# First batch of the attention: diagonal-scaled transposes, V stationary, x produced transposed

## The chip, the cores and the metric

The kernel runs on one core of one Trainium2 chip, as a single program. Engines are named as in the profile: PE (TensorE matmuls), PEld (its weight loads), DVE (VectorE), ACT (ScalarE), POOL (GpSimd) and SP (SyncE, here a DMA queue). The metric is the device time of one execution in microseconds (us), as the median over runs; the kernel before takes 684.7 us (three runs, 682.42 to 688.06).

## What is computed

Three stages follow one another: a banded attention, a SiLU feed-forward network, and a mixture of eight experts of which each token uses one. The change touches the attention alone (2 batches, 8 heads, 768 positions, 64 columns a head; the first 8 key positions are seen by all queries, and each query sees 96 positions back):

```python
scores = scale * np.matmul(q, k.transpose(0, 1, 3, 2)) + bias     # bias falls with distance
scores = np.where(keep, scores, -1000000000.0)
a = np.exp(scores - np.max(scores, axis=-1, keepdims=True))
a = a / (np.sum(a, axis=-1, keepdims=True) + 1e-09)
x = np.matmul(a, v)                       # then x: (1536 tokens, 512) goes on
h = x @ w_in
g = h * (1.0 / (1.0 + np.exp(-h)))
x = g @ w_out                             # then the experts
```

## The kernel before, in words

The 1536 tokens are 12 tiles of 128; tiles 0 to 5 are the first batch, tiles 6 to 11 the second. The attention of a tile is done in four steps of two heads each, called slots: slot s is tile s//4, head pair s%4. The first batch is slots 0 to 23 (`SB=24`) and runs ahead of everything else, by `slot_b`; the second batch runs between the matmuls of the feed-forward network, by `slot`, and isn't touched.

A pair of heads goes through a pipeline over four slots. In slot s the code issues, in this order (the instructions of an engine run in the order in which they are issued, under `manual_schedule`):

- `emit_tr` for slot s-2: four PE transposes against the identity (two heads, two key blocks of 128; tile 0 has one block, so two transposes), then ACT's copy of the result to SBUF (L187);
- `emit_tb` for the first head of slot s: DVE adds the bias table to the scores and takes the row maximum (L159);
- `emit_exp` for slot s-1: two ACT exponentials with row sums in `ss` (L169);
- one step of the decoding of a weight (`dec_op`, DVE, from slot 8 on; the weights arrive as 64-bit words and three DVE steps make them 32-bit);
- `emit_tb` for the second head, and `emit_mx`, which scales the maximum (L162); then `emit_qk` for slot s+1: the scores of two heads, each a float32 matmul over 64 rows and 256 columns (L150);
- `glob_k` (POOL copies the global keys, L138), then `emit_pv` for slot s-3: four float32 matmuls in which the transposed weights are the stationary operand and 64 columns of V stream (L197). They fill `pvt[n]`, 128 tokens by 512.

When a tile's fourth pair is through, `emit_rs` makes the inverse sums on DVE (L206, L207), `emit_fin` multiplies `pvt` by them into `xa` (DVE, L211), and one slot later `emit_xt` transposes `xa` by four PE transposes (L218); ACT copies that to `xT` (L222), and DVE makes the rest of the split of `xT` into two float32r parts (L223). The feed-forward network reads `xT` as its streaming operand (L292).

PSUM banks of the pipeline come in turn from five (`abank`, L112). A float32 matmul that isn't a transpose shows in the trace as two instructions (88 matmuls at L197 give 176 rows, 48 at L150 give 96), a transpose as one. POOL also computes the bias tables in the first slots (`tab_heads`, L109, in slots 1, 2, 4, 5, 6, 9 by `TAB`). `WPL` (L40) holds the slots after which nine loads of weights are issued on the SP queue.

The first feed-forward matmul (L292) follows slot 23 on PE. Slots 24 to 26, which only finish the pipeline, stand between the matmuls of its first steps. In those steps DVE decodes the weights that are left.

Of the kernel before, what the change touches and what calls it, by code (L numbers as in the profile page):

```python
# [10 lines left out]
F32 = mybir.dt.float32  # L11
# [5 lines left out]
AF = mybir.ActivationFunctionType  # L17
ALU = mybir.AluOpType
AX = mybir.AxisListType
P = 128  # L20
# [3 lines left out]
def kernel(ctx, tc, qk, v, n_global, n_local, w_in, w_out, wg, w1, w2, out):  # L24
    nc=tc.nc
    B,NT=v.shape[0],v.shape[1]
    H=8; D=64; KC=4; FB=16; NTT=B*NT; LAG=2; LASTF=2; HB=6; PAIR=256; PX=4
# [4 lines left out]
    SB=24  # L32
# [4 lines left out]
    WL=4  # L37
    LOPB=(1,2,3)
    LATE=(0,1)
    WPL=(2,4,6,8,10,12,14,17,20)  # L40
    WPS=(12,15,18,21,23)
    TAB=(1,2,4,5,6,9)
    const=ctx.enter_context(tc.tile_pool(name="const",bufs=1,side="left"))
# [1 line left out]
    attn=es_a.enter_context(tc.tile_pool(name="attn",bufs=1,side="right"))  # L45
# [11 lines left out]
    ident=const.tile([P,P],F32,name="ident")  # L57
# [4 lines left out]
    def own_first(n): return n%3==1  # L62
# [76 lines left out]
    def glob_v(n):  # L139
        if n%NT in (0,NT-1): return  # L140
        if 4*n<SB: G.tensor_copy(vpr4[0:32,n%3,0:512],vpr4[0:32,(n-1)%3,0:512])
        else: V.tensor_copy(vpr[0:32,n%3],vpr[0:32,(n-1)%3])
# [8 lines left out]
    def emit_tb(n,hp,j):  # L151
        i=n%NT; h=2*hp+j; q=qp.pop((n,hp,j))
        if j==0: tt[n,hp]=attn.tile([P,2,2,P],F32,tag="t",name="t",bufs=3)
        t=tt[n,hp]
        if h==0:
            mx[n]=attn.tile([P,H],F32,tag="mx",name="mx",bufs=2); ss[n]=attn.tile([P,H],F32,tag="ss",name="ss",bufs=2)
        sl=slice(0,2) if i else slice(0,1)
        tb=tabs[:,3:4,h,:] if i==0 else (tabs[:,1::-1,h,:] if i==1 else tabs[:,1:3,h,:]) if own_first(n) else tabs[:,0:2,h,:] if i==1 else tabs[:,2:0:-1,h,:]
        V.tensor_tensor_reduce(out=t[:,j,sl],in0=q[:,sl],in1=tb,scale=1.0,scalar=-3e38,op0=ALU.add,op1=ALU.max,accum_out=mx[n][:,h:h+1])  # L159
    def emit_mx(n,hp):  # L160
        h=2*hp+1
        V.tensor_scalar(out=mx[n][:,h-1:h+1],in0=mx[n][:,h-1:h+1],scalar1=-0.125,scalar2=float(np.log(1024.0)),op0=ALU.mult,op1=ALU.add)  # L162
    def emit_exp(n,hp):
        i=n%NT
        t=tt[n,hp]
        ce=1 if i==0 else 2
        for j in range(2):
            h=2*hp+j
            A.activation(out=t[:,j,:ce],in_=t[:,j,:ce],func=AF.Exp,scale=0.125,bias=mx[n][:,h:h+1],accum_out=ss[n][:,h:h+1])  # L169
# [4 lines left out]
    def emit_l(n,hp):  # L174
        t=tt.pop((n,hp)); x=hl.pop((n,hp)); nch=ce=1 if n%NT==0 else 2
        (G if hp in LOPB else V).tensor_tensor(out=x[:,:,1],in0=t[:,:,:ce],in1=x[:,:,0],op=ALU.subtract)
        y=attn.tile([P,2,2,nch,P],F16,tag="pT",name="pT",bufs=3)
        pT[n,hp]=y
        S.dma_start_transpose(out=y.rearrange("p a b c d -> p (a b c) d"),in_=x.rearrange("p a b c d -> p (a b c d)"))
    def emit_tr(n,hp):  # L180

        t=tt.pop((n,hp)); ce=1 if n%NT==0 else 2
        m=abank([P,2,ce,P],"tp")
        for j in range(2):
            for c in range(ce): T.transpose(m[:,j,c],t[:,j,c],ident)
        y=attn.tile([P,2,ce,P],F32,tag="pT",name="pT4",bufs=3); pT[n,hp]=y
        A.activation(out=y,in_=m,func=AF.Copy)  # L187
    def emit_pv(n,hp):
        i=n%NT; ce=1 if i==0 else 2
        if hp==0: pvt[n]=ps.tile([P,H,D],F32,tag="pv" if 4*n>=SB or n%2 else "s1",name="pv",bufs=1)  # L190
        y=pT.pop((n,hp))
        vb=[n%3] if ce==1 else [n%3,(n-1)%3] if own_first(n) else [(n-1)%3,n%3]
        for j in range(2):
            h=2*hp+j
            for c in range(ce):
                if 4*n<SB:
                    T.matmul(pvt[n][:,h,:],y[:,j,c,:],vpr4[:,vb[c],h*D:(h+1)*D],start=(c==0),stop=(c==ce-1))  # L197
                    continue
                seq=[(0,0),(0,1),(0,2),(1,0),(1,1)]
                for k,(a,m) in enumerate(seq):  # L200
                    T.matmul(pvt[n][:,h,:],y[:,j,a,c,:],vpr[:,vb[c],m,h*D:(h+1)*D],start=(c==0 and k==0),stop=(c==ce-1 and k==4))
    rs={}
    def emit_rs(n,k):
        if k==0:
            rs[n]=attn.tile([P,H,1],F32,tag="rs",name="rs",bufs=2)
            V.tensor_scalar(out=rs[n][:,:,0],in0=ss[n],scalar1=1024.0e-9,scalar2=None,op0=ALU.add)  # L206
        else: V.reciprocal(out=rs[n],in_=rs[n])  # L207
    def emit_fin(n):
        r=rs.pop(n)
        xa=attn.tile([P,H,D],F32,tag="hl" if 4*n<SB else "t",name="xa",bufs=2 if 4*n<SB else 3)  # L210
        V.tensor_tensor(out=xa,in0=pvt[n],in1=r.to_broadcast([P,H,D]),op=ALU.mult)  # L211
        xas[n]=xa
    xas={}
    def emit_xt(n):
        xa=xas.pop(n)
        m=abank([P,KC,P],"ms")
        for k in range(KC):
            T.transpose(m[:,k,:],xa[:,2*k:2*k+2,:].rearrange("p a d -> p (a d)"),ident)  # L218
        c,u=divmod(n,2)
        if u==0: xT[c]=mp.tile([P,2,KC,256],F32R,tag="xT",name="xT",bufs=3)  # L220
        sl=xT[c][:,:,:,u*P:(u+1)*P]
        A.activation(out=sl[:,0],in_=m,func=AF.Copy)  # L222
        V.tensor_tensor(out=sl[:,1],in0=m,in1=sl[:,0],op=ALU.subtract)  # L223
# [616 lines left out]
    def slot_b(s):  # L840

        ev=[]
        n,hp=divmod(s,4); n1,h1=divmod(s-1,4); n2,h2=divmod(s-2,4); n3,h3=divmod(s-3,4)
        def a_():
            if s<SB-3: want(min(s+WL,SB-1))
            elif s<SB: want(s+3)
            if 0<=s-2<SB: emit_tr(n2,h2)
            if s==0:
                for j in range(2): emit_qk(n,hp,j)
            if s<SB: emit_tb(n,hp,0)  # L850
            if 0<=s-1<SB: emit_exp(n1,h1)
        ev.append(a_)
        def a2():
            if s<SB: emit_tb(n,hp,1); emit_mx(n,hp)
            if s+1<SB:
                for j in range(2): emit_qk(*divmod(s+1,4),j)
        ev.append(a2)
        def b_():
            if s<SB: glob_k(n,hp)
            if 0<=s-3<SB:  # L860
                emit_pv(n3,h3)
                if h3==3: glob_v(n3)
            if h3==3 and 0<=s-3<SB: emit_rs(n3,0); emit_rs(n3,1)
            if fin: emit_xt(fin.pop())
            if s==0: table(slice(0,3))
            for k in range(2):
                if s==TAB[k]:
                    for h in range(4*k,4*k+4): tab_heads(slice(0,2),slice(0,2),(h,))
            for k in range(4):
                if s==TAB[2+k]:  # L870
                    for h in range(2*k,2*k+2): tab_heads(slice(2,3),slice(2,3),(h,))
        ev.append(b_)
        def e2():
            if h3==3 and 0<=s-3<SB: emit_fin(n3); fin.append(n3)
            if hp==3 and n+1<NTT and s<SB: load_v(n+1)
        ev.append(e2)
        return ev
# [144 lines left out]
```

## Time and profile before

| what | value |
|---|---|
| median of 3 runs | 684.7 us |
| the profiled execution, its own time | 692.54 us |
| its span, first to last instruction | 690.7 us |
| PE busy | 647.9 us (94%) |
| PE weight loads | 541.4 us (78%) |
| DVE busy | 384.3 us (56%) |
| ACT busy | 303.3 us (44%) |
| POOL busy | 204.8 us (30%) |

The page gives each engine's busy time and the share of the span. A view by stretches gives busy time, granted clock and DMA share of chosen microseconds. The timeline gives instructions in order of time, equal neighbours merged into one row with their count; the difference of two rows' starts is what the first one cost the engine. A matmul's recorded length overlaps its neighbour's, so on PE starts are read and not lengths.

### The profile page before, as it was taken

To read this page: it belongs to the slowest core of one execution; us is meant where nothing else is said; L and a number is where in the kernel's file an instruction comes from. 1 tells how busy PE (TensorE), PEld (TensorE's weight loads), DVE (VectorE), ACT (ScalarE), POOL (GpSimd) and SP (SyncE) were. 2 spreads that over 40 slices of the span, in tenths; PEclk is the share of its full clock that TensorE was granted. 3 is DMA by queue.
4 is the path that set the end of the run, shared out by engine and by line. 5 is a ranking of instruction groups with operands and counts; after the bars stand their busy time and mean duration, and the time that the engine had idled before them with its cause. 6 is when DMAs were issued, how large, how long until landed. Compare 5 with 4: busy or idle time off the path is not lost. (4 is left out here: it accounts for less than half of the span.)

```text
span 690.7 us, 11869 instructions
## 1 busy us (share of the span) xinstructions
PE 647.9 (94%) x3990; PEld 541.4 (78%) x3990; DVE 384.3 (56%) x1013; ACT 303.3 (44%) x789; POOL 204.8 (30%) x230
## 2 busy tenths in 40 slices
PE   2999998999989989999999999889799999999995
PEld 1677787888878868888888989778688888888883
DVE  3344444999963555555535334474274387779750
ACT  2444444334434434433343232444266376766641
POOL 5412120344421133212211101172443244434311
PEclk9999999999999999999999999999899999999998
DMA  7132223377433788547355735951685456776600
GB/s 256 34 106 78 76 76 127 120 222 217 159 115 105 81 165 169 138 93 167 93 129 92 131 92 76 245 164 31 198 267 177 154 175 216 238 264 220 215 18 18
DMA packets 83671, 98.75 MB, mean 143 GB/s; under 512 B 35547, under 2 KB 49883, under 8 KB 83602
## 3 DMA queue, kind: packets, MB, share of 16 engines
q1 hardware_dynamic: 76850, 86.69, 46.5%
q0 software_dynamic: 3312, 8.08, 3.6%
q10 hardware_dynamic: 3440, 3.15, 1.5%
q8 instruction: 33, 0.54, 0.3%
q14 instruction: 36, 0.29, 0.1%
HBM read 81.85 MB, written 11.52 MB: 135 GB/s over the span
## 5 line engine op out<-in xcount | busy, mean ns | idle before, releaser
L292 PEld LDWEIGHTS s<-xT,wi 128*128 128x128 f32 x1152 | 150.6, 194 | 19.2 <-DVE g L301 12.3
L292 PE MATMUL s<-xT,wi 128*128 128x256 f32 x1152 | 156.3, 288 | 6.3 <-DVE g L301 5.4
L297 DVE SCALAR_TENSOR_TENSOR s<-u,s 128x256 f32<-128x256 f32 x96 | 39.8, 426 | 104.1 <-ACT u L296 103.7
L296 ACT ACTIVATE u<-s 128x256 f32<-128x256 f32 x96 | 35.2, 380 | 114.3 <-PE s L292 110.5
L307 PE MATMUL s<-woh,g 128*128 128x512 f32 x192 | 81.8, 426 | 0.0
L458 DVE TENSOR_TENSOR uq<-qr,uq 128x512 fp32r<-128x512 f32 x81 | 76.3, 957 | 8.0 <-ACT uq L457 4.4
L308 PE MATMUL s<-woh,g 128*128 128x512 f32 x192 | 77.7, 405 | 0.0
L150 PE MATMUL qkp<-ring 64*128 64x256 f32 (+1 forms) x192 | 60.0, 543 | 15.1 <-DMA ring<-in_qk_dram 12.3
L457 ACT ACTIVATE uq<-qr 128x512 fp32r<-128x512 f32 x112 | 66.4, 625 | 7.6 <-DMA qr<-in_w_dram 7.6
L301 DVE TENSOR_TENSOR g<-s,g 128x256 fp32r<-128x256 f32 x96 | 39.3, 422 | 31.8 <-ACT g L300 24.0
L458 POOL TENSOR_TENSOR uq<-qr,uq 128x512 fp32r<-128x512 f32 x31 | 41.0, 1331 | 53.8 <-ACT uq L457 50.3
L300 ACT ACTIVATE g<-s 128x256 fp32r<-128x256 f32 x96 | 35.7, 380 | 47.2 <-DVE s L297 46.7
L607 PE MATMUL y<-uq,hh 128*128 128x512 f32 (+6 forms) x136 | 55.7, 410 | 0.0
L608 PE MATMUL y<-uq,hh 128*128 128x512 f32 (+6 forms) x136 | 54.0, 397 | 0.0
L609 PE MATMUL y<-uq,hh 128*128 128x512 f32 (+6 forms) x136 | 54.0, 397 | 0.0
L309 PE MATMUL s<-wolr,g 128*128 128x512 f32 x128 | 52.0, 406 | 0.2 <-DMA wolr<-wlo_d 0.2
L150 PEld LDWEIGHTS qkp<-ring 64*128 64x128 f32 x192 | 26.8, 247 | 30.2 <-DMA ring<-in_qk_dram 9.9
L197 PEld LDWEIGHTS pv<-vpr,pT 128*128 128x128 f32 x176 | 36.9, 308 | 13.0 <-issue 13.0
L169 ACT ACTIVATE t<-t,mx 128x256 f32<-128x256 f32 (+1 forms) x96 | 45.7, 480 | 0.4 <-DVE mx L162 0.4
L599 ACT ACTIVATE hh<-h 128x224 fp32r<-128x224 f32 (+6 forms) x64 | 23.3, 363 | 49.6 <-DVE h L597 29.0
L307 PEld LDWEIGHTS s<-woh,g 128*128 128x128 f32 x192 | 37.5, 195 | 9.5 <-ACT u L296 1.7
L600 DVE SCALAR_TENSOR_TENSOR hh<-h,hh 128x224 fp32r<-128x224 f32 (+6 forms) x64 | 25.3, 395 | 32.6 <-ACT hh L599 29.6
(211 smaller groups left out, 1134.2 us busy)
## 6 DMA issues: line engine op xcount, KB each, us to landing
qr<-in_w_dram SPq DMA_DIRECT2D x128, 256.0 KB
wolr<-wlo_d SPq DMA_DIRECT2D x64, 256.0 KB
wiraw<-in_w_in_dram SPq DMA_DIRECT2D x16, 512.0 KB
wraw<-in_w_out_dram SPq DMA_DIRECT2D x13, 512.0 KB
wlo_d<-wol SPq DMA_DIRECT2D x16, 256.0 KB
xs<-xr SPq DMA_DIRECT2D x6, 513.0 KB
ring<-in_qk_dram SPq DMA_DIRECT2D x12, 256.0 KB
ring<-in_qk_dram ACTq DMA_DIRECT2D x10, 256.0 KB
```

Source lines behind the costliest of these rows:

```text
L150: T.matmul(q[:,sl],w[:,z,1],w[:,z:z+1,0] if i==0 else w[:,0:3:2,0] if z==0 else w[:,z-1:z+1,0],start=True,stop=True)
L169: A.activation(out=t[:,j,:ce],in_=t[:,j,:ce],func=AF.Exp,scale=0.125,bias=mx[n][:,h:h+1],accum_out=ss[n][:,h:h+1])
L292: T.matmul(t,w[:,ww,kc,:],x[:,xx,kc,:],start=(k==0),stop=(k==11)); k+=1
L297: V.scalar_tensor_tensor(out=t,in0=u,scalar=1.0,in1=t,op0=ALU.add,op1=ALU.mult)
L307: T.matmul(s2p[u][k],g[:,0,sl],wh,start=(f==0),stop=False)
L308: T.matmul(s2p[u][k],g[:,1,sl],wh,start=False,stop=False)
L309: T.matmul(s2p[u][k],g[:,0,sl],wl,start=False,stop=(f==FB-1))
L457: A.activation(out=t[:,0],in_=r,func=AF.Copy)
L458: (G if (i%2 if pool is None else pool) else V).tensor_tensor(out=t[:,1],in0=r,in1=t[:,0],op=ALU.subtract)
L607: T.matmul(o,g[:,0,sl],w[:,0],start=(f==0),stop=False)
L608: T.matmul(o,g[:,1,sl],w[:,0],start=False,stop=False)
L609: T.matmul(o,g[:,0,sl],w[:,1],start=False,stop=(f==7))
```

## The change

It concerns the first batch alone.

- New `emit_dg` for slot s-1, issued in slot s behind `emit_mx`: DVE adds the constant to the two row sums and inverts them (two small instructions a slot), and POOL multiplies the identity by each head's inverse sums, one 128 by 128 instruction a head: a diagonal matrix `dg`, float32, in two buffers.
- `emit_tr` no longer transposes against the identity: it is an ordinary float32 matmul with the exponentials as the stationary operand and `dg` streaming. What comes out is the transposed weights, already divided by their sums. ACT's copy of it is issued behind the exponentials of slot s-1 and no longer ahead of them.
- `emit_px` takes the place of `emit_pv`: V (64 columns) is the stationary operand, the transposed weights (128 columns) stream. The two heads of a pair write to partitions 0 to 63 and 64 to 127 of the same PSUM columns, in turn. x comes out transposed, tile by tile, and goes to `xT` at once by `put_xt` (the ACT copy and the DVE subtraction as before, read from the matmul's own bank).
- Gone from the first batch: `emit_rs`, `emit_fin` and the four transposes of `emit_xt` for each of six tiles.
- `WPL`: the loads of weights on the SP queue come up to two slots later.

```diff
-    WPL=(2,4,6,8,10,12,14,17,20)
+    WPL=(4,6,8,10,12,14,16,18,20)
...
+    def emit_dg(n,hp):
+        s=ss[n][:,2*hp:2*hp+2]
+        V.tensor_scalar(out=s,in0=s,scalar1=1024.0e-9,scalar2=None,op0=ALU.add)
+        V.reciprocal(out=s,in_=s)
+        d=attn.tile([P,2,P],F32,tag="hl",name="dg",bufs=2); dg[n,hp]=d
+        for j in range(2): G.tensor_scalar(out=d[:,j],in0=ident,scalar1=s[:,j:j+1],scalar2=None,op0=ALU.mult)
...
-            for c in range(ce): T.transpose(m[:,j,c],t[:,j,c],ident)
+            for c in range(ce): T.matmul(m[:,j,c],t[:,j,c],d[:,j],start=True,stop=True)
...
-        A.activation(out=y,in_=m,func=AF.Copy)
+        return y,m
+    def emit_px(n,hp):
+        i=n%NT; ce=1 if i==0 else 2
+        if hp==0: pvt[n]=ps.tile([P,KC,P],F32,tag="pv" if n%2 else "s1",name="px",bufs=1)
...
+        for c in range(ce):
+            for j in range(2):
+                h=2*hp+j
+                T.matmul(pvt[n][j*D:(j+1)*D,hp,:],vpr4[:,vb[c],h*D:(h+1)*D],y[:,j,c,:],start=(c==0),stop=(c==ce-1))
+    def emit_xx(n):
+        put_xt(n,pvt[n])
...
-                    T.matmul(pvt[n][:,h,:],y[:,j,c,:],vpr4[:,vb[c],h*D:(h+1)*D],start=(c==0),stop=(c==ce-1))
...
-            if 0<=s-2<SB: emit_tr(n2,h2)
+            if 0<=s-2<SB: y,m=emit_tr(n2,h2)
...
             if 0<=s-1<SB: emit_exp(n1,h1)
+            if 0<=s-2<SB: A.activation(out=y,in_=m,func=AF.Copy)
...
             if s<SB: emit_tb(n,hp,1); emit_mx(n,hp)
+            if 0<=s-1<SB: emit_dg(n1,h1)
...
-                emit_pv(n3,h3)
-                if h3==3: glob_v(n3)
-            if h3==3 and 0<=s-3<SB: emit_rs(n3,0); emit_rs(n3,1)
-            if fin: emit_xt(fin.pop())
+                emit_px(n3,h3)
+                if h3==3: glob_v(n3); emit_xx(n3)
...
-            if h3==3 and 0<=s-3<SB: emit_fin(n3); fin.append(n3)
```

The order on PE around the end of a tile, in the middle of the first batch. The names are the tiles written and read; a count behind a row counts matmuls of the code. Before:

```order
L150 MATMUL qkp<-ring_78 128x256 x2
L197 MATMUL pv<-vpr,pT_383 128x64 x4
L218 MATMUL ms<-ident,xa 128x128 x4
L185 MATMUL tp<-ident,t 128x128 x4
L150 MATMUL qkp<-ring_78 128x256 x2
L197 MATMUL pv<-vpr,pT_412 128x64 x4
```

And with the change:

```order
L150 MATMUL qkp<-ring_78 128x256 x2
L204 MATMUL px<-pT_416,vpr 64x128 x4
L193 MATMUL tp<-dg,t 128x128 x4
L150 MATMUL qkp<-ring_78 128x256 x2
L204 MATMUL px<-pT_447,vpr 64x128 x4
```

The four transposes of `xa` are gone; the transposes of the weights have become matmuls against `dg`, and the product with V has changed its operands' places.

The order on POOL in the first slots, before (the tables of L109 stand together):

```order
L109 TENSOR_SCALAR tabs<-wk 128x128 x6
L109 TENSOR_SCALAR tabs<-wk 128x2x128 x8
L138 COPY ring_78<-ring_78 128x32
L109 TENSOR_SCALAR tabs<-wk 128x128 x2
L138 COPY ring_78<-ring_78 128x32
```

And with the change:

```order
L109 TENSOR_SCALAR tabs<-wk 128x128 x6
L187 TENSOR_SCALAR dg<-ident,ss 128x128 x2
L109 TENSOR_SCALAR tabs<-wk 128x2x128 x4
L187 TENSOR_SCALAR dg<-ident,ss 128x128 x2
L109 TENSOR_SCALAR tabs<-wk 128x2x128 x4
L187 TENSOR_SCALAR dg<-ident,ss 128x128 x4
```

The diagonals of slots 0 and 1 now stand ahead of each group of four tables, and those of slots 2 and 3 behind the eighth.

The order on DVE at the end of a tile, with the change (`ISA` at L159 is the addition of the bias with its maximum, and the read of that maximum):

```order
L162 TENSOR_SCALAR mx<-mx 128x2
L184 TENSOR_SCALAR ss<-ss 128x2
L185 RECIPROCAL ss<-ss 128x2
L241 TENSOR_TENSOR xT<-px,xT 128x4x128
L159 ISA t,mx<-qkp,tabs 128x256
L159 ISA mx 128x1
```

The two small instructions for `dg` stand behind each slot's `mx`, and at the end of a tile the subtraction for `xT` follows them directly, ahead of the next slot's bias.

## Rows read from the trace of the kernel before

**Rows 1.** Busy time by stretch, attention of the first batch: us, engines, PEclk, DMA, GB/s

```profile
20.00:101.40 81.40, 81.40 (x322) 60.88 (x323) 34.89 (x132) 35.69 (x109) 17.82 (x43) 1.00 0.21 68
```

**Rows 2.** Timeline of PE, one slot: start, us, engine, line, operation, operands, count

```profile
79.06 1.97 PE L197 MATMUL pv<-vpr,pT 128*128 128x64 f32 x8
80.82 1.06 PE L185 MATMUL tp<-ident,t 128*128 128x128 f32 x4
81.81 1.23 PE L150 MATMUL qkp<-ring 64*128 64x256 f32 x4
82.97 0.47 PE L197 MATMUL pv<-vpr,pT 128*128 128x64 f32 x1
```

**Rows 3.** Timeline of PE, the same operations after the first feed-forward matmuls

```profile
104.93 0.60 PE L185 MATMUL tp<-ident,t 128*128 128x128 f32 x4
105.36 1.00 PE L197 MATMUL pv<-vpr,pT 128*128 128x64 f32 x8
...
107.53 1.00 PE L197 MATMUL pv<-vpr,pT 128*128 128x64 f32 x8
108.34 3.11 PE L292 MATMUL s<-xT,wi 128*128 128x256 f32 x24
```

**Rows 4.** Busy time by stretch, one with a recorded lower clock (PEclk 0.50)

```profile
208.50:211.80 3.30, 3.30 (x10) 2.52 (x9) 1.34 (x3) 1.43 (x3) 0.69 (x1) 0.50 0.24 62
```

**Rows 5.** Timeline of PE, second feed-forward matmuls inside that stretch, and earlier

```profile
119.19 0.39 PE L307 MATMUL s<-woh,g 128*128 128x512 f32 x1
119.42 0.39 PE L308 MATMUL s<-woh,g 128*128 128x512 f32 x1
...
208.72 0.63 PE L307 MATMUL s<-woh,g 128*128 128x512 f32 x1
209.14 0.63 PE L308 MATMUL s<-woh,g 128*128 128x512 f32 x1
```

**Rows 6.** Timeline of PE, scores of a pair of heads of the second batch

```profile
226.95 0.70 PE L150 MATMUL qkp<-ring 64*128 64x256 f32 x4
227.59 0.18 PE L376 MATMUL gr<-geb,upper 128*128 128x8 bf16 x1
```

**Rows 7.** Timeline of PE, start of slots 4 and 6, and end of the stage

```profile
20.20 0.63 PE L185 MATMUL tp<-ident,t 128*128 128x128 f32 x2
...
25.45 1.06 PE L185 MATMUL tp<-ident,t 128*128 128x128 f32 x4
...
101.43 3.66 PE L292 MATMUL s<-xT,wi 128*128 128x256 f32 x24
```

**Rows 8.** Timeline of POOL and ACT in the first slots: tables, and slot 0's exponentials

```profile
13.96 6.88 POOL L109 TENSOR_SCALAR tabs<-wk 128x256 bf16<-128x256 f32 x8 [2.41 <-DVE wk L107]
...
13.04 0.18 ACT L169 ACTIVATION_READ_ACCUMULATOR t<-t,mx 128x1 f32 x1
```

**Rows 9.** Groups by line and form, 20 to 100 us: count, busy us, mean ns

```profile
L169 ACT ACTIVATE t<-t,mx 128x256 f32<-128x256 f32 x37 | 18.3, 498 | 0.0
L159 DVE CUSTOM_DVE_ANT_1 t<-qkp,tabs 128x256 f32<-128x256 f32 x39 | 16.0, 418 | 13.8 <-PE qkp L150 13.8
L187 ACT ACTIVATE pT<-tp 128x512 f32<-128x512 f32 x18 | 10.7, 597 | 33.9 <-PE tp L185 33.9
L162 DVE TENSOR_SCALAR mx<-mx 128x2 f32<-128x2 f32 x20 | 4.4, 220 | 0.7
L109 POOL TENSOR_SCALAR tabs<-wk 128x128 bf16<-128x128 f32 x8 | 4.2, 528 | 0.3
L223 DVE TENSOR_TENSOR xT<-ms,xT 128x512 fp32r<-128x512 f32 x4 | 2.8, 692 | 13.4 <-ACT xT L222 13.4
L248 DVE SCALAR_TENSOR_TENSOR dct<-wiraw,dct 128x512 int32<-128x512 int32 x3 | 2.1, 691 | 0.0
L207 DVE RECIPROCAL rs<-rs 128x8 f32<-128x8 f32 x5 | 1.0, 203 | 0.2
```

**Rows 10.** Timeline of PE, last tile's transposes between the feed-forward's first steps

```profile
114.44 0.66 PE L218 MATMUL ms<-ident,xa 128*128 128x128 f32 x4 [2.15 <-DVE xa L211]
```

More of the change, by code (lines that the diff above doesn't have):

```diff
@@ L179, in emit_l @@
         S.dma_start_transpose(out=y.rearrange("p a b c d -> p (a b c) d"),in_=x.rearrange("p a b c d -> p (a b c d)"))
+    dg={}
+    def emit_dg(n,hp):
[4 more added lines that the diff above has]
+        for j in range(2): G.tensor_scalar(out=d[:,j],in0=ident,scalar1=s[:,j:j+1],scalar2=None,op0=ALU.mult)
     def emit_tr(n,hp):
-        t=tt.pop((n,hp)); ce=1 if n%NT==0 else 2
+        t=tt.pop((n,hp)); d=dg.pop((n,hp)); ce=1 if n%NT==0 else 2
         m=abank([P,2,ce,P],"tp")
         for j in range(2):
-            for c in range(ce): T.transpose(m[:,j,c],t[:,j,c],ident)
+            for c in range(ce): T.matmul(m[:,j,c],t[:,j,c],d[:,j],start=True,stop=True)
         y=attn.tile([P,2,ce,P],F32,tag="pT",name="pT4",bufs=3); pT[n,hp]=y
-        A.activation(out=y,in_=m,func=AF.Copy)
+        return y,m
+    def emit_px(n,hp):
+        i=n%NT; ce=1 if i==0 else 2
+        if hp==0: pvt[n]=ps.tile([P,KC,P],F32,tag="pv" if n%2 else "s1",name="px",bufs=1)
+        y=pT.pop((n,hp))
+        vb=[n%3] if ce==1 else [n%3,(n-1)%3] if own_first(n) else [(n-1)%3,n%3]
+        for c in range(ce):
[4 more added lines that the diff above has]
+        put_xt(n,pvt[n])
     def emit_pv(n,hp):
         i=n%NT; ce=1 if i==0 else 2
-        if hp==0: pvt[n]=ps.tile([P,H,D],F32,tag="pv" if 4*n>=SB or n%2 else "s1",name="pv",bufs=1)
+        if hp==0: pvt[n]=ps.tile([P,H,D],F32,tag="pv",name="pv",bufs=1)
         y=pT.pop((n,hp))
@@ L195, in emit_pv @@
             for c in range(ce):
-                if 4*n<SB:
-                    T.matmul(pvt[n][:,h,:],y[:,j,c,:],vpr4[:,vb[c],h*D:(h+1)*D],start=(c==0),stop=(c==ce-1))
-                    continue
                 seq=[(0,0),(0,1),(0,2),(1,0),(1,1)]
@@ L209, in emit_fin @@
         r=rs.pop(n)
-        xa=attn.tile([P,H,D],F32,tag="hl" if 4*n<SB else "t",name="xa",bufs=2 if 4*n<SB else 3)
+        xa=attn.tile([P,H,D],F32,tag="t",name="xa",bufs=3)
         V.tensor_tensor(out=xa,in0=pvt[n],in1=r.to_broadcast([P,H,D]),op=ALU.mult)
@@ L218, in emit_xt, with put_xt @@
             T.transpose(m[:,k,:],xa[:,2*k:2*k+2,:].rearrange("p a d -> p (a d)"),ident)
+        put_xt(n,m)
+    def put_xt(n,m):
         c,u=divmod(n,2)
```

## The prediction

> **What bounds the kernel now.** I read the view by stretches first. From 20 to 101.4 us, where the first batch's attention runs, PE is busy all of the 81.40 us, while DVE has 34.89, ACT 35.69 and POOL 17.82 [rows 1]. So the price of this stage is PE's, and what DVE, ACT and POOL do there is hidden as long as it comes in time.
>
> The timeline of PE then gives the slot. Starts are read: eight products with V from 79.06 to 80.82 (1.76 us), four transposes from there to 81.81 (0.99), four score instructions to 82.97 (1.16), 3.91 us in all [rows 2]. The same operations after the first feed-forward matmuls cost half: four transposes from 104.93 to 105.36 are 0.108 us each, eight products from 107.53 to 108.34 are 0.101 us each [rows 3], against 0.99 / 4 (with a change of shape, 0.14, in it; 0.21 without) and 1.76 / 8 = 0.22 in the slot. The reader is to see a clock here which the granted clock's column doesn't show: it reads 1.00 for the stage [rows 1]. Where a lower clock is recorded (0.50, that is 1.2 GHz) [rows 4], matmuls of 512 columns start 0.42 us apart, and 0.23 elsewhere [rows 5], the same ratio. I take it that the stage runs at 1.2 GHz to 101.4 us although PE never idles, and that the chip went to 2.4 GHz in the first train of feed-forward matmuls, which stream without a gap.
>
> So the change has two sides: it gives PE more work in a slot, and another kind of work, which may bring the higher clock 70 us earlier.
>
> **PE's work in a slot.** Neither a 128-column float32 matmul that isn't a transpose nor one with 64 stationary columns is in the trace. The bounds are its neighbours: 64 streaming columns at 0.22 us at the low clock and 0.101 at the high one [rows 2, 3]; 256 columns, two halves of the rows side by side, 1.16 / 2 = 0.58 us a pair, and 0.64 / 2 = 0.32 at the high clock (226.95 to 227.59) [rows 6]. A third of the way between them, 128 columns cost 0.34 us at the low clock and 0.174 at the high one.
>
> - Transposes: four (four instructions) become four matmuls of two instructions: 8 x 0.174 = 1.39 us and 0.07 for the change of shape, 1.46 (low clock 8 x 0.34 + 0.14 = 2.86). Lower bound, if each goes like a transpose: 8 x 0.108 = 0.86.
> - Scores: unchanged, 0.64 (low 1.16).
> - Products with V: eight instructions as before, now of 128 columns. The two heads write different halves of the partitions. If these go side by side as the score pairs do, 4 x 0.174 = 0.70 (low 1.36); if one after the other, 1.39 (low 2.72). I take side by side, since the only half-array matmuls in the trace do so.
> - Gone: four transposes per tile, 0.86 us at the low clock, 0.21 a slot.
>
> Sum: 2.80 us at the high clock (3.49 with the heads in turn), 5.38 at the low one (6.74). Before, the mean slot is 75.98 / 18 = 4.22 us: slot 6 starts at 25.45, the feed-forward network at 101.43 [rows 7].
>
> The Trainium skill ("TensorE: Matmul & The Clock Gate", part 4, PE-mode transpose) says that transposes don't count as activity for the clock gate as other matmuls do. The trace agrees so far as 80 us of a busy PE with transposes in every slot didn't raise the clock [rows 1, 2]. By that rule the change, which leaves no transpose in the stage, ends in the case I forecast, 672 us; without the rise it is the third rival, 709 us.
>
> **The chain behind a slot.** The new way from exponentials to transposed weights is two exponentials with their reads, about 1.1 us (0.498 each), two small DVE instructions (0.220 and 0.203 from the nearest rows), the first diagonal on POOL: 0.53, as a 128 by 128 table takes [rows 9]. A diagonal of slot s is needed two PE slots later, 5.6 us. The longest way round there: the transposes of slot s-2 (1.46), scores (0.64), about 0.3 to reach DVE, two additions of the bias (0.42 each) with a decoding step between them (0.69) and the maximum's scaling (0.22), the two small instructions (0.42), the diagonal (0.53): 5.1 us for two slots, under 5.6. So it hides, with 0.5 us to spare. The exponentials no longer wait behind ACT's copy (0.597), which is what the copy's new place saves; the product with V that needs the copy is one slot later.
>
> At a tile's end it doesn't hide. There, ACT's copy of x (0.6) and the subtraction (0.69) [rows 9] stand on DVE ahead of the next slot's bias; from the tile's last product on: 0.3 + 0.6 + 0.69 + 0.84 + 0.22 + 0.42 + 0.53 = 3.6, with a decoding step 4.3, and the diagonal is wanted after 2.8. That leaves 0.8 to 1.5 us of idle PE once in four slots, 0.3 a slot. So **3.1 us a slot** at the high clock. The 48 diagonals are 25 us of POOL, hidden in the stage while they come in time.
>
> **The start.** Here POOL isn't hidden. Its eight tables run from 13.96 to 20.84, 0.86 each [rows 8]. Slot 0's exponentials end at 13.22 [rows 8]; behind the bias of slot 1 and the small instructions on DVE, 1.7 us (an estimate from their durations, [rows 9]), the diagonals take POOL from 14.9 to 16.0, ahead of the tables now. Then four tables to 19.4, two diagonals to 20.5, four tables to 23.9, the first diagonal of slot 2 at 24.5. Slot 4's transposes, which need it, started at 20.20 [rows 7]: 4.3 us late. Slots 4 and 5 (one key block, half of a slot's matmuls) at the low clock: 1.5 + 1.16 + 0.68 = 3.3 each, so slot 6 starts at 31.1 and not at 25.45. Five diagonals stand ahead of slot 4's transposes: if they cost nothing the start gains 2.6 us back, at 0.86 (a table of twice the elements) it loses 1.7.
>
> **The rest.** The weights' loads move past loads of V on the SP queue and come up to two slots later; the first is decoded four slots after its issue, over 12 us, and in the stage the queues move 68 GB/s [rows 1]: no cost; if they came late, the decoding on DVE, and the bias behind it, would wait. The last tile's transposes go, and with them 2.15 us of idle PE [rows 10]; but slots 24 and 25 cost more there, 2 x (1.39 - 0.43), so I count nothing. Behind it everything moves with the start of the feed-forward network, whose first steps wait for DVE's decoding, not for an absolute time.
>
> **The sum.** Slots 6 to 23 at 3.1 are 55.8 us, less 0.64 since slot 23 has no scores, plus 2.3 if one slot is still at the low clock: 57.5. The feed-forward network starts at 31.1 + 57.5 = 88.6 us and not at 101.4, 12.8 us earlier. The profiled execution goes from 692.5 to 679.7 us; it lies 7.8 us over the median of the three runs, which goes from 684.7 to **672 us**.
>
> **Rivals.**
>
> 1. *The heads' products go in turn.* Then a slot is 3.49 + 0.2 = 3.7 us; 66.6 - 0.64 + 3.0 for a slot at the low clock, from 32.4 (slots 4 and 5 cost 0.7 more each): the network starts at 101.4, **684 us**, no change. For it: no half-column matmul is in the trace. Against it: the half-row pairs do run side by side. The Trainium skill ("TensorEngine Tiling (Array Packing)", key properties) says that tiles run in parallel but that a change of the tiling mode drains the engine. The trace shows the price of a change, 0.14 us at the low clock [rows 2]; one more of them a slot is within my sum's error.
> 2. *A longer chain.* If POOL's diagonals or DVE's small instructions are late in each slot and not once a tile, the slot is bound by them. From 3.9 us a slot ((101.4 - 31.1 + 0.6) / 18) nothing is gained. It would take 0.8 us more in each slot than I count; it ends in the same place, 680 to 690.
> 3. *The clock stays at 1.2 GHz.* Then 18 slots of 5.38 are 96.8 us, the network starts 25 us later: **709 us**, with the heads in turn 735. It is slower as soon as six slots more than I count run at the low clock (12.8 / 2.3). For it: a busy PE alone hasn't raised the clock before [rows 1]. Against it: the work that streams in a slot more than doubles, and the train that did raise it was of ordinary matmuls.
>
> **How the numbers follow.** My forecast has a chance of 0.55, with 663 to 678 us of its own; rivals 1 and 2 together 0.23 (678 to 691); rival 3 0.17 (700 to 735); a faster end than 663 (transposing matmuls at their lower bound, 2.2 us of work a slot, and the chain then binds at 2.55: 659) 0.05. The range for 8 in 10 leaves out rival 3: 662 to 692. A change of 1% (6.8 us) is about what a measurement of this kernel can tell from none: faster 0.60, within 1% 0.22, slower 0.18.
>
> **What would show it.** Transposing matmuls 0.17 us apart from about 33 us on (0.34: rival 3); products with V in pairs with starts a few ns apart (else rival 1); slots of 3.1 us; PE idle of about a microsecond before the transposes once a tile, released by POOL (in every slot: rival 2); slot 4 at about 24.5 us; the first L310 near 89 us. The clock decides the sign; I am wrong first of all if it doesn't rise.

## The result, and the profile after

The changed kernel takes 665.5 us (median, 664.2 to 666.7) and the kernel before, run beside it, 685.2 us (682.4 to 688.1): a ratio of 0.971, with a 95% interval of 0.967 to 0.976. It is faster by 19.7 us. The forecast was 672 us, a gain of 12.7.

| | before | after |
|---|---|---|
| time of the profiled execution (its span) | 692.5 us (690.7) | 666.7 us (665.0) |
| slot 6's first transposing instruction | 25.45 us | 29.19 us |
| mean of slots 6 to 23 | 4.22 us | 2.85 us |
| first feed-forward product | 101.43 us | 80.47 us |
| from there to the 97th instruction of that line (its fifth group of 24) | 25.4 us | 23.7 us |
| from the first feed-forward product to the end | 589.3 us | 584.5 us |

The mean slot after is (80.47 - 29.19) / 18. The first feed-forward product thus comes 20.96 us earlier, and its first steps are another 1.7 us shorter. That leaves 3.1 us of the 25.8 us between the two profiled executions, which no edit explains: the part behind the attention differs by such amounts from one execution to the next (below).

The view by stretches, for the attention of the first batch (columns as in [rows 1], whose 81.40 us it answers):

```profile
20.00:80.40 60.40, 52.95 (x384) 36.51 (x382) 35.32 (x154) 35.97 (x108) 39.94 (x76) 0.97 0.32 101
```

PE is busy for 52.95 of 60.40 us and no longer all the time, DVE and ACT have about as much work as before, and POOL has gone from 17.82 to 39.94 us, since it writes the diagonals. PEclk, 0.97, has a fall to 0.50 in it: for 3.4 us of the stage the lower clock is recorded, the rest reads 1.00. The fall makes one slot long: from 58.73 to 62.46 us, 3.73 us.

The timeline of PE, slot 6 and its successors, then two slots in the middle, a slot that waits at a tile's end, and the first feed-forward steps (to compare with [rows 2, 3, 7, 10]):

```profile
23.17 1.38 PE L193 MATMUL tp<-dg,t 128*128 128x128 f32 x4 [1.61 <-POOL dg L187]
...
29.19 2.08 PE L193 MATMUL tp<-dg,t 128*128 128x128 f32 x8
31.19 1.21 PE L150 MATMUL qkp<-ring 64*128 64x256 f32 x4
...
32.70 1.16 PE L193 MATMUL tp<-dg,t 128*128 128x128 f32 x8
33.79 0.70 PE L150 MATMUL qkp<-ring 64*128 64x256 f32 x4
34.42 0.66 PE L204 MATMUL px<-pT,vpr 128*64 128x128 f32 x8
...
47.39 1.29 PE L193 MATMUL tp<-dg,t 128*128 128x128 f32 x8 [1.31 <-POOL dg L187]
...
49.93 1.29 PE L193 MATMUL tp<-dg,t 128*128 128x128 f32 x8
51.15 0.70 PE L150 MATMUL qkp<-ring 64*128 64x256 f32 x4
51.78 0.66 PE L204 MATMUL px<-pT,vpr 128*64 128x128 f32 x8
52.37 1.16 PE L193 MATMUL tp<-dg,t 128*128 128x128 f32 x8
53.46 0.70 PE L150 MATMUL qkp<-ring 64*128 64x256 f32 x4
...
80.47 3.12 PE L310 MATMUL s<-xT,wi 128*128 128x256 f32 x24
83.44 1.05 PE L193 MATMUL tp<-dg,t 128*128 128x128 f32 x8
84.42 0.66 PE L204 MATMUL px<-pT,vpr 128*64 128x128 f32 x8
...
86.26 1.29 PE L193 MATMUL tp<-dg,t 128*128 128x128 f32 x8 [1.19 <-POOL dg L187]
```

The clock is seen in the durations. Eight transposing instructions take 2.00 us from 29.19 (to 31.19) and 1.09 us from 32.70 (to 33.79). The score instructions behind the second eight take 0.63 us (33.79 to 34.42) and not 1.16 [rows 2]. The lower level held to about 32.3 us, into slot 6, and not to the stage's end. From 52.37 on one reads a slot's parts: transposing 1.09 (52.37 to 53.46), scores 0.63 (51.15 to 51.78), products with V 0.59 (51.78 to 52.37), 2.31 in all.

The wait at a tile's end (PE idle 1.31 us ahead of 47.39) has this chain behind it, from the timeline of ACT, DVE and POOL: ACT's copy of x, DVE's subtraction, which holds up the next slot's bias on DVE, and then the diagonals, for which POOL waits until DVE has the sums:

```profile
43.47 0.60 ACT L240 ACTIVATE xT<-px 128x512 fp32r<-128x512 f32 x1 [0.57 <-PE px L204]
44.10 0.69 DVE L241 TENSOR_TENSOR xT<-px,xT 128x512 fp32r<-128x512 f32 x1 [1.65 <-ACT xT L240]
...
46.73 1.18 POOL L187 TENSOR_SCALAR dg<-ident,ss 128x128 f32<-128x128 f32 x2 [1.94 <-DVE ss L185]
```

### The profile page after: what moved, and what is told of

Read it like the earlier page. It is cut to its first block, busy times and chain, and to the rows that moved or that the text cites. A ratio compares the mean times of both kernels' runs of the same rounds, so it can differ in the third digit from the quotient of the medians.

```text
span 665.0 us, 12071 instructions
## 1 busy us (share of the span) xinstructions
PE 616.9 (93%) x4054; PEld 514.8 (77%) x4054; DVE 387.7 (58%) x1043; ACT 303.7 (46%) x789; POOL 232.6 (35%) x278
## 4 chain that ended last, share of the span: by engine, by line
PE 74%; issue 8%; DVE 6%; DMA 5%; ACT 3%; POOL 3%; SPq 0%; ACTq 0%; POOLq 0%; DVEq 0%
PE s L310 19%; PE s L325 6%; PE s L326 6%; PE s L327 6%; PE h L602 5%; PE qkp L150 5%; PE y L625 4%; PE y L627 4%; PE y L626 4%; PE h L608 4%; PE tp L193 3%; PE h L603 3%; PE pv L217 2%; PE px L204 1%; PE gl L370 1%
## 5 line engine op out<-in xcount | busy, mean ns | idle before, releaser
L476 DVE TENSOR_TENSOR uq<-qr,uq 128x512 fp32r<-128x512 f32 x81 | 74.2, 932 | 8.2 <-ACT uq L475 5.0
L150 PE MATMUL qkp<-ring 64*128 64x256 f32 (+1 forms) x192 | 48.3, 454 | 10.8 <-DMA ring<-in_qk_dram 8.2
L193 PE MATMUL tp<-dg,t 128*128 128x128 f32 x176 | 31.3, 322 | 14.3 <-POOL dg L187 14.1
L159 DVE CUSTOM_DVE_ANT_1 t<-qkp,tabs 128x256 f32<-128x256 f32 x80 | 32.7, 417 | 16.4 <-PE qkp L150 16.3
```

What stands on the lines that cost most here:

```text
L150: T.matmul(q[:,sl],w[:,z,1],w[:,z:z+1,0] if i==0 else w[:,0:3:2,0] if z==0 else w[:,z-1:z+1,0],start=True,stop=True)
L193: for c in range(ce): T.matmul(m[:,j,c],t[:,j,c],d[:,j],start=True,stop=True)
L476: (G if (i%2 if pool is None else pool) else V).tensor_tensor(out=t[:,1],in0=r,in1=t[:,0],op=ALU.subtract)
```

## Experiments

Each has the times of the same session beside it. The kernel before had a median of 690.7, 690.8 and 690.3 us in the three sessions (runs e, f and g), more than the 685.2 above, with single runs from 675.6 to 694.7; so small differences are read between runs of one session only.

**e1: transposes as products, nothing else.** From the kernel before, one line:

```diff
-            for c in range(ce): T.transpose(m[:,j,c],t[:,j,c],ident)
+            for c in range(ce): T.matmul(m[:,j,c],t[:,j,c],ident,start=True,stop=True)
```

> The kernel before with one edit: its transposes of the weights become ordinary float32 matmuls against the identity; nothing else is moved. Theory 1 (the gain is the clock, and the transposes kept it low): the granted clock rises in the first batch near 30 us, matmuls against the identity start 0.11 us apart, a slot falls from 4.22 to about 2.9 us, 662 to 668 us. Theory 2 (the gain is less PE work in a slot: no transposes of x, V stationary): the clock stays low, four instructions more a slot at 0.21 us, 18 x 0.85 = 15 us more, about 700 us.

Measured: 674.7 us (673.0 to 675.0), ratio 0.976 (0.972 to 0.980). The view by stretches, and a slot of PE's timeline:

```profile
30.50:79.50 49.00, 48.07 (x356) 39.23 (x355) 31.59 (x117) 30.92 (x91) 12.03 (x24) 1.00 0.32 103
...
48.67 1.11 PE L185 MATMUL tp<-ident,t 128*128 128x128 f32 x8
49.71 0.70 PE L150 MATMUL qkp<-ring 64*128 64x256 f32 x4
50.34 1.10 PE L197 MATMUL pv<-vpr,pT 128*128 128x64 f32 x8
51.28 0.89 PE L185 MATMUL tp<-ident,t 128*128 128x128 f32 x6
```

Scores take 0.63 us (49.71 to 50.34) and the old products with V 0.94 (50.34 to 51.28), against 1.16 and 1.76 in [rows 2]: the same instructions in the same order at half the duration, because four transposes a slot were written as four products (eight instructions). The slot is 2.61 us. The first feed-forward product comes at 79.6 us, earlier than in the changed kernel. So the clock alone shortens this stage by as much as the whole change does. The diagonals and the transposed x aren't needed for it. The mechanism is theory 1's; its 662 to 668 us were missed by 6.7 us (g1, below, asks where they went).

**e2: the changed kernel with transposes.** The inverse sums are multiplied into the weights on POOL, and the transposes come back:

```diff
-        d=attn.tile([P,2,P],F32,tag="hl",name="dg",bufs=2); dg[n,hp]=d
-        for j in range(2): G.tensor_scalar(out=d[:,j],in0=ident,scalar1=s[:,j:j+1],scalar2=None,op0=ALU.mult)
+        t=tt[n,hp]; ce=1 if n%NT==0 else 2
+        for j in range(2): G.tensor_scalar(out=t[:,j,:ce],in0=t[:,j,:ce],scalar1=s[:,j:j+1],scalar2=None,op0=ALU.mult)
...
-            for c in range(ce): T.matmul(m[:,j,c],t[:,j,c],d[:,j],start=True,stop=True)
+            for c in range(ce): T.transpose(m[:,j,c],t[:,j,c],ident)
```

> The changed kernel with its transposes put back (against the identity, one instruction each); the inverse sums are multiplied into the exponentials on POOL, two instructions of up to 128 by 256 a slot in place of the two diagonals. Theory 1 (the clock rises because the transposes became matmuls): the clock stays low to the feed-forward network, transposes 0.21 us apart, a slot 0.99 + 1.16 + about 1.1 = 3.2 us or what POOL's two instructions make of it, 670 to 676 us. Theory 2 (V stationary with 128 streaming columns is enough for the clock): the clock rises as in the changed kernel, transposes 0.11 us apart, 662 to 667 us.

Measured: 677.7 us (676.3 to 680.7), ratio 0.982 (0.978 to 0.987); first feed-forward product at 83.7 us. By stretches:

```profile
42.20:49.10 6.90, 4.27 (x35) 2.31 (x33) 4.80 (x22) 4.38 (x12) 5.12 (x9) 1.00 0.35 119
49.20:52.40 3.20, 3.20 (x17) 1.82 (x18) 1.37 (x5) 1.57 (x5) 3.13 (x4) 0.50 0.68 247
52.50:62.70 10.20, 7.10 (x55) 3.73 (x53) 6.26 (x28) 6.37 (x18) 8.57 (x12) 1.00 0.42 133
```

The higher clock comes 10 us later than after the change, at 42 us, and is lost again: PE, faster then, idles for POOL's longer multiplications (4.27 busy of 6.90 us), the clock falls, PE is busy without a gap at 0.50, and the clock rises again. So transposes in a slot don't forbid the rise: with the weights' transposes kept, the products with V changed and x's transposes gone, it comes and goes. It was held, but for the 3.4 us named above, where products stand in the transposes' place and PE seldom waits (e1 and the changed kernel); e4 will show products without transposes and a clock that falls all the same, as PE waits. Whether it is the transposes or the waits that lose the higher clock here, e2 doesn't tell, since POOL's work on the weights adds waits of its own. Neither theory's time came: 677.7 us is above both ranges.

**e3: products with V in turn.** The loops over heads and key blocks are exchanged, so that both products of one head stand ahead of the other head's:

```diff
-        for c in range(ce):
-            for j in range(2):
+        for j in range(2):
+            for c in range(ce):
```

> The changed kernel with the two heads of a product with V one after the other (both key blocks of a head first), so that neighbours in the code write the same half of the partitions. Theory 1 (side by side is what makes the product cheap): the eight instructions take about 0.9 us and not 0.58, 0.3 us a slot in the two thirds of the slots that don't wait for POOL, 669 to 672 us. Theory 2 (PE's waits for the diagonals absorb it): the slot stays at 2.85 us and the time within 2 us of 665.5.

Measured: 666.0 us (665.0 to 668.5), ratio 0.965 (0.960 to 0.970). PE's timeline:

```profile
51.10 0.66 PE L204 MATMUL px<-pT,vpr 128*64 128x128 f32 x8
51.70 1.16 PE L193 MATMUL tp<-dg,t 128*128 128x128 f32 x8
```

The eight instructions still take 0.60 us, as in the written order before. In the single records the starts still come in pairs, 13 ns apart (7 ns in the changed kernel), where full-width products start 0.111 us apart: eight of those would take 0.89 us. A record doesn't name the half or the head that it belongs to: a pair may be one instruction of each half, which would mean here that one head's passes the other's, or the two instructions of one product. The starts alone don't decide it. In any case the edit did not undo what it was meant to undo: the products overlap in either order, and a price for products in turn was not measured. Theory 2's time came, but not for its reason.

**e4: the copy first.** ScalarE's copy of the transposed weights goes back ahead of the next exponentials:

```diff
-            if 0<=s-2<SB: y,m=emit_tr(n2,h2)
+            if 0<=s-2<SB:
+                y,m=emit_tr(n2,h2)
+                A.activation(out=y,in_=m,func=AF.Copy)
...
-            if 0<=s-2<SB: A.activation(out=y,in_=m,func=AF.Copy)
```

> The changed kernel with ACT's copy of the transposed weights issued ahead of the next exponentials again. Theory 1 (the order on ACT closes a chain of one slot): transposing matmuls 1.0, reach of ACT 0.3, copy 0.5, two exponentials 1.1, two small DVE instructions 0.35, a diagonal 0.6, 3.9 us a slot and not 2.85, waits of PE for POOL in every slot, 18 us more, about 683 us. Theory 2 (the order on ACT is hidden, as ACT is busy 60% of the stage): within 2 us of 665.5.

Measured: 701.3 us (699.4 to 702.5), ratio 1.014 (1.010 to 1.019): slower than before the change. First feed-forward product at 110.5 us. The view of waits from 32 to 80 us (waiting engine, tile and line, whom it waited for, us, times, longest), and two slots of PE:

```profile
DVE ss L184 <- ACT t L169: 25.3, 11, 3.7
PEld tp L193 <- POOL dg L187: 15.4, 10, 1.9
PE tp L193 <- POOL dg L187: 12.2, 10, 1.7
...
45.17 1.29 PE L193 MATMUL tp<-dg,t 128*128 128x128 f32 x8 [1.70 <-POOL dg L187]
...
49.38 2.08 PE L193 MATMUL tp<-dg,t 128*128 128x128 f32 x8 [1.16 <-POOL dg L187]
```

Transposes, copy, exponentials, sums, diagonals and the next transposes now stand in one ring, and it takes 4.2 us. PE waits in each slot, the clock falls again and again (mean 0.82 from 20 to 110.5 us), and at the lower clock the ring is longer still, 5.00 us (49.38 to 54.38). I had expected 3.9 us and 683. The 18 slots from 30.95 us on take 4.42 us in the mean, where the changed kernel's take 2.85: 28 us, of which 24 are the ring at 4.2 us and the rest the clock. The start adds 1.8 us, and the part behind the stage, 589.8 us, is no longer than in other traces (593.2 in e1).

**f1 to f4: what PE still waits for.** f1 is the changed kernel again. f2 writes the diagonals on VectorE; f3 issues x's copy and subtraction one slot later; f4 does both, with VectorE's diagonals in the first tile alone.

```diff
-        for j in range(2): G.tensor_scalar(out=d[:,j],in0=ident,scalar1=s[:,j:j+1],scalar2=None,op0=ALU.mult)
+        for j in range(2): V.tensor_scalar(out=d[:,j],in0=ident,scalar1=s[:,j:j+1],scalar2=None,op0=ALU.mult)
```

```diff
+            if lx: emit_xx(lx.pop())
...
-                if h3==3: glob_v(n3); emit_xx(n3)
+                if h3==3: glob_v(n3); lx.append(n3)
```

> The changed kernel unchanged, as the base for the runs beside it. Every theory: 665.5 us as in the comparison before, within 2 us; first feed-forward product at about 80.5 us, and the waits of TensorE for the diagonals at the start (2.56 and 1.61 us) and at each tile's end (1.1 to 1.6 us) as before.

> The diagonals of the first batch are written by VectorE instead of GpSimd. Theory 1 (GpSimd's 1.2 us for two diagonals is on the path while the first tiles start, where a step has one key block and TensorE waits 2.56 and 1.61 us): the start is 3 to 4 us shorter, the later steps the same, since VectorE's work in a step then is some 2.0 us against TensorE's 2.3, and the time is 661 to 663. Theory 2 (VectorE, which in every fourth step also has the decoding of weights, becomes the longer chain): the waits move from the diagonals to the sums L184 and the first feed-forward product comes at 80 us or later; 665 to 668.

> The copy and the subtraction that turn a finished tile's x into its two parts are issued one step later, behind the next step's diagonals, so that neither ScalarE's 692 ns nor VectorE's 691 ns stand ahead of the next step's exponentials, sums and diagonals. Theory 1 (these two are what TensorE waits for at a tile's end): the five waits of 1.1 to 1.6 us at tile ends go, the first feed-forward product comes 5 to 6 us earlier (75 us), and the time is 660. Theory 2 (the wait moves one step on, since the same work stands in the next step): the stage ends within 1.5 us of 80.5 and the time is 664 to 667.

> Both edits: diagonals of the first tile alone on VectorE, those of the other tiles on GpSimd, and x one step later. If both theories 1 hold: first feed-forward product at 71 to 73 us and 656 to 658 us. If the stage is shorter but later stages take the gain back: 71 to 73 us at the first product and 661 to 666 us in all. If neither holds: 665.

Measured: f1 668.8 us (665.8 to 672.9), ratio 0.970 (0.964 to 0.976); f2 660.8 us (658.9 to 666.1), 0.960 (0.954 to 0.965); f3 667.8 us (665.5 to 669.3), 0.969 (0.964 to 0.974); f4 663.3 us (659.6 to 663.5), 0.961 (0.957 to 0.966). First feed-forward products at 80.05, 72.65, 79.43 and 73.46 us. PE's timeline of f2, start and three slots:

```profile
18.63 1.22 PE L193 MATMUL tp<-dg,t 128*128 128x128 f32 x4
...
24.50 2.08 PE L193 MATMUL tp<-dg,t 128*128 128x128 f32 x8
...
45.24 1.16 PE L193 MATMUL tp<-dg,t 128*128 128x128 f32 x8
46.33 0.70 PE L150 MATMUL qkp<-ring 64*128 64x256 f32 x4
46.96 0.66 PE L204 MATMUL px<-pT,vpr 128*64 128x128 f32 x8
47.55 1.16 PE L193 MATMUL tp<-dg,t 128*128 128x128 f32 x8
...
49.85 1.16 PE L193 MATMUL tp<-dg,t 128*128 128x128 f32 x8
```

Slot 6 starts 4.7 us earlier than after the change (24.50 against 29.19), and between the tile ends a slot is 2.31 us, PE's own work. At a tile's end PE still waits, 0.69 to 2.36 us, 5.6 us in all four. The whole gain of the stage, 7.4 us against f1, arrives at the end (8.0 us). VectorE needs 0.48 us for two diagonals where GpSimd needs 1.18 to 1.20, and it is busy for 42.45 of 52.60 us then (DVE, the third of the busy times by stretch), so it still isn't the bound:

```profile
20.00:72.60 52.60, 46.99 (x372) 33.24 (x372) 42.45 (x184) 34.74 (x104) 14.32 (x31) 1.00 0.35 111
```

Theory 1 holds for f2, and the gain was larger than I expected, since GpSimd's diagonals were on the path in the later slots too. How much of it is theirs takes a look at the clock. f1 has the same fall as the changed kernel (a slot of 3.91 us from 58.35, where one without it takes 2.44) and f2 has none, which is 1.5 us; in f2, in turn, slot 6 stays at the lower clock longer (3.76 us against 3.11). That leaves about 1.9 us of the 2.7 that f2 gains behind the start.

f1 itself missed its expectation: 668.8 us, 3.3 above 665.5, with the first feed-forward product at 80.05 as expected.

f3 is a miss. PE's waits at tile ends only move one slot on and shrink a little, and a new one stands ahead of the first feed-forward product:

```profile
38.63 1.29 PE L193 MATMUL tp<-dg,t 128*128 128x128 f32 x8 [0.98 <-POOL dg L187]
49.27 1.29 PE L193 MATMUL tp<-dg,t 128*128 128x128 f32 x8 [0.93 <-POOL dg L187]
...
79.43 3.13 PE L310 MATMUL s<-xT,wi 128*128 128x256 f32 x24 [1.37 <-DVE xT L241]
```

That the waits move with x's copy and subtraction agrees with the chain shown above; theory 2 holds, its time but for 0.8 us. Late x is late for the feed-forward network, which waits 1.37 us for it. f4 ends between f2 and f1, nearest to its second case. Its slot 6 starts at 24.51 us, as in f2, so VectorE in the first tile brings the 4.7 us of the start; the other 1.9 us that its first product gains on f1 are no more than the clock gives, which rises earlier (slot 6 takes 2.47 us and not 3.11) and has no fall in the stage.

**g1 to g4.** g1 is e1 once more, g2 the changed kernel with the old list of slots for the loads of weights (`WPL=(2,4,6,8,10,12,14,17,20)`; the expectation below calls it decoding, but the list moves the loads), g3 is f2 with late x, g4 is f2 with the copy first as in e4.

> The kernel of e1 once more (the kernel before, its transposes of the first batch written as matrix products with the identity), to see what the rest of the change adds to the clock. Theory 1 (the rest is worth only what the traces show, 1.9 us of the first feed-forward steps and about 0.5 us of the stage; what else stood between e1 and e3 is the spread of the later stages, in which two traces of the changed kernel differ by 4.4 us): 2 to 5 us above the changed kernel, 669 to 674. Theory 2 (the later stages of this kernel are slower for a reason of their own): 675 or more, and the span from the first feed-forward product to the end 592 us or more again, against 584.5 and 588.9 of the changed kernel.

> The changed kernel with the old list of steps at which weight decoding is placed. Theory 1 (the list moves idle work): within 2 us of the changed kernel, 665 to 669, first feed-forward product at 80 to 81 us. Theory 2 (decoding in the first steps, where tiles start, is in the way): first product at 82 us or later, 668 to 671.

> Diagonals of all tiles on VectorE and x one step later. Theory 1 (TensorE's own 2.3 us now bounds a step, and the waits of up to 2.6 us for the exponentials at the tile ends are due to x's copy ahead of them on ScalarE): first feed-forward product at 69 to 71 us, time 657 to 659. Theory 2 (as in f3, the waits only move): 72 to 73 us and 659 to 662.

> Diagonals on VectorE, and ScalarE's copy of the transposed weights ahead of the next exponentials again (as in e4). Theory 1 (the order closes a chain through a single step whatever engine writes the diagonals: copy 0.60, two exponentials 1.18, sums and reciprocal 0.33, first diagonal 0.28, products 1.16, hand-overs some 0.2 to 0.4, together 3.7 to 4.0 us against 2.3): steps of 3.7 us or longer, first feed-forward product at 92 to 100 us, time 680 to 690. Theory 2 (in e4 it was GpSimd's two 0.60 us diagonals and the low clock that made it slow): steps of 2.6 us, first product at 78 us at the latest, time 663 to 667.

Measured: g1 671.5 us (669.4 to 675.6), g2 670.2 us (667.4 to 672.7), g3 665.4 us (664.1 to 666.7), g4 689.3 us (685.2 to 693.9). I compare medians here.

g1: first feed-forward product at 79.2 us, 588.7 us from there to the end. The changed kernel has 584.5 and 588.9 in its two traces. Theory 2 falls. What e1 lacks is what the traces show, 25.6 us in the first feed-forward steps (23.7 after the change), with the wait of [rows 10] still in them. Of the 8.7 us between e1 and e3, 1.2 stand at the first product (79.58 against 78.38) and 1.9 in those steps; the other 5.6 lie in the later stages, and I take them for the spread that two traces of one kernel show there.

g2: first product at 79.8 us, and 670.2 us, 1.2 above the range of theory 1; by these two numbers the list is worth nothing. The start says otherwise. The first row is ACT's first instruction for the later tables after the change, the others are g2's:

```profile
9.64 0.52 ACT L102 ACTIVATE wk<-ii 128x384 f32<-128x384 int32 x1 [5.11 <-POOL tabs L109]
...
11.48 0.52 ACT L102 ACTIVATE wk<-ii 128x384 f32<-128x384 int32 x1 [6.90 <-POOL tabs L109]
14.90 1.21 POOL L187 TENSOR_SCALAR dg<-ident,ss 128x128 f32<-128x128 f32 x2 [3.44 <-DVE ss L185]
31.03 1.55 PE L193 MATMUL tp<-dg,t 128*128 128x128 f32 x8
```

With the old list the start is 1.84 us later, from ACT's instruction on (it stands behind two issues of loads for the scores on ACT's queue, which come later): slot 4 at 25.01 against 23.17, slot 6 at 31.03 against 29.19. In all four kernels with the old list (before, e1, g1, g2) that instruction starts at 11.42 to 11.53 us, in the ten with the new one at 9.58 to 9.67. Why weights on the SP queue hold up issues on ACT's isn't shown. Behind the start the clock gives the 1.84 us back in g2: slots 6 to 23 take 48.78 us there, 49.18 in e3, 50.84 in f1 and 51.28 after the change. In g2 and e3 the clock rises sooner within slot 6 (2.49 and 2.75 us for it, 3.51 after the change) and doesn't fall later. So the list is worth 1.84 us at the start, and the stage's end in a single trace can't tell 2 us. e1 and g1 with the new list were not run.

g3: the stage is the shortest of all (71.1 us), and the time is 4.6 us above f2. Its network waits 1.79 us for x before its first product; the part behind that product takes 593.8 us against f2's 587.3, with eight recorded falls of the clock against four. Both theories for g3 had expected less. Those two runs are from different sessions, so how much of the 4.6 us is the edit's stays open.

g4: PE's timeline and DVE's wait, from 32 to 80 us:

```profile
DVE ss L184 <- ACT t L169: 15.7, 12, 2.2
PE tp L193 <- DVE dg L187: 12.5, 13, 1.3
...
47.10 1.13 PE L193 MATMUL tp<-dg,t 128*128 128x128 f32 x8 [1.32 <-DVE dg L187]
48.16 0.70 PE L150 MATMUL qkp<-ring 64*128 64x256 f32 x4
48.79 0.66 PE L204 MATMUL px<-pT,vpr 128*64 128x128 f32 x8
50.77 0.68 PE L193 MATMUL tp<-dg,t 128*128 128x128 f32 x4 [1.32 <-DVE dg L187]
```

The ring takes 3.67 us (47.10 to 50.77) at the higher clock, as worked out beforehand, and the first product comes at 97.4 us. So it is the order on ScalarE that closes the ring, whichever engine writes the diagonals; it costs 24.7 us at the first feed-forward product against f2 (72.65), and 28.5 in the medians, which are of two sessions. The mean slot is 3.91 us ((97.39 - 26.92) / 18), and the time is that of the kernel before.

## Why the prediction was right, and where its numbers were off

**The clock.** The step that decides the sign held: the stage ran at the lower level, the rise comes at about 32 us, near the 33 that I had named, and e1 shows that the rise is the cause, not a companion. The place of the rise had no working behind it: one slot at the lower clock was an assumption, and the runs put the rise anywhere from 20.8 us (g3) to 42 (e2). That it fitted is luck. The Trainium skill ("TensorE: Matmul & The Clock Gate", part 4) says that transposes don't count as activity for the clock gate as other matmuls do; e1 agrees, since there only that was changed (four transposes for four products, which are eight instructions) and the clock rose at 30.2 us; whether the kind of instruction or their doubled number did it, e1 doesn't separate. e2 sets a limit to reading it too strongly: with transposes in every slot the clock did rise, at 42 us.

**Transposing products: mis-sized.** I took 0.174 us for an instruction of 128 float32 columns, a third of the way between 64 and 256 columns, and named 0.108, a transpose's, as the lower bound. They start 0.111 us apart (0.213 at the lower clock), so the lower bound was right and the operation is 1.09 us, not 1.46. The straight line between 64 and 256 columns was the fault: from 64 columns (0.101 in [rows 3]) to 128 the price rose by 0.01 us. By the same error the lower-clock slot was priced at 5.38 us: slot 6 to slot 7 took 3.51 with its end already at the higher clock, and the parts are 2.00, 1.14 to 1.16 and 1.05 (e2, 37.53 to 38.59 us), about 4.2, just the slot before. **Rival 3's** 709 us was thus wrong too: by these parts, an estimate, the stage without the rise would have lost the 3.7 us of its start and little else. No run kept the clock down with the changed work. A chance of 0.17 stood on a size that no row supported.

**Products with V.** Side by side, as taken: 0.59 us a slot where 0.70 was counted. **Rival 1's** price is out, and by e3 the other written order doesn't bring it about either; which two instructions overlap stays open.

**Slots.** 2.31 us of work where 2.80 stood, 2.85 with the waits where 3.1 stood. This is the largest part of the extra gain: 18 slots take 51.3 us, not 57.5. The wait at the tile's end came as worked out, 1.07 to 1.64 us, released by POOL, by the chain that was named (x's copy, subtraction, bias, sums, diagonal). But a diagonal takes 0.60 us, not the 0.53 of a table, and with PE's slot down to 2.31 us there is no spare time of 0.5 us left: f2 shows about 1.9 us of GpSimd's diagonals on the path after the start. **Rival 2**, the longer chain, is thus there in part, and e4 and g4 show what it costs in full: its break-even, 3.9 us a slot, is g4's, at the time of the kernel before.

**The start.** Slot 4 at 23.17 us (24.5 predicted, 20.20 before) and slot 6 at 29.19 (31.1 predicted): diagonals between POOL's tables, as worked out. f2 confirms the cause by taking it away. The 1.9 us by which slot 6 came earlier than predicted are the list of loads: with the old one, g2, POOL's first diagonals start at 14.90 and slot 6 at 31.03, as predicted to 0.1 us.

**The rest.** "I count nothing" for the first feed-forward steps was 1.7 us short: the wait of 2.15 us [rows 10] is gone, one of 1.19 us has come, and the transposing products of the two slots there cost 0.98 and 1.23 us (83.44 to 84.42, 86.26 to 87.49) where I had 1.39 each. For the list of loads "no cost" was put at nothing where it gains 1.84 us at the start (g2).

**The sum.** 88.6 us was predicted for the first feed-forward product and 80.47 measured: 1.9 us from the start, 6.2 from the slots. With the 1.7 us of the first steps the traces are 9.8 us better than forecast, the median only 6.5: the profiled execution before lay 7.8 us over its median, the one after 1.2, so that the time was met better than its parts by luck. The condition of the fastest case, transposing products at their lower bound, to which I had given 0.05, came true; its 659 us didn't, since the tile's ends and the fall of the clock make the slot 2.85 us and not 2.55. The chance of 0.60 for faster was low, mainly because of rival 3's price.

## What to carry to other kernels

Compare the durations of the same instruction in two places of a trace: a stage in which PE is busy without a gap may be running at half clock, and writing its transposes as products with the identity, one line, can bring the higher level. When PE gets twice as fast, look at once for the engine that was hidden until then (here GpSimd's diagonals, 8 us when VectorE writes them), and for rings that go through one slot, which the order of two instructions on a third engine opens or closes. Before a small edit is called idle, look where its first instructions start: the list of loads moved the start by 1.84 us, and the clock hid it in the stage's end. Price an unknown instruction at both bounds in every rival, too, above all in the one that would decide against the change.

## What was not expected of the hardware

- A float32 product of 128 by 128 with a 128-column moving operand costs PE about the same per instruction as a transpose: 0.111 us at the higher clock (a transpose 0.108), 0.213 at the lower (0.21); a product is two instructions, a transpose one.
- Products whose stationary operands have 64 columns, with results in two halves of the partitions, overlap: eight instructions in 0.59 to 0.60 us, starts in pairs, also where the written order puts one half's instructions first (e3).
- The granted clock's column doesn't show the lower level ahead of the first rise in these traces. From 20 to 32 us it reads 1.00 after the change, while eight transposing instructions take 2.00 us there:

```profile
20.00:32.00 12.00, 10.39 (x44) 6.32 (x42) 3.54 (x21) 4.51 (x16) 9.93 (x19) 1.00 0.13 45
```

- The part behind the first feed-forward product took 584.5 and 588.9 us in two traces of the same kernel, so that a single trace doesn't tell 4 us there. Up to that product, too, the clock's rises and falls differ from trace to trace: slots 6 to 23 took 48.78 to 51.28 us in g2, e3, f1 and after the change.
